# Retention in streamed 128-token units, GpSimd pass rewritten, engine orders pinned: a kernel of attention and ELU feed-forward on one core

## The chip, the cores and the metric

One core of a Trainium2 chip. The time is that of one execution on the device in microseconds (us), as the median of the runs that are quoted with it. "Span" is the time from the first to the last instruction of the profiled execution, and is about 2 us shorter than the time of that execution.

The engines: PE is TensorE, PEld its weight loads, DVE is VectorE, ACT is ScalarE, POOL is GpSimd, SP is the engine whose queue issues most DMAs. PSUM is the memory that the kernels use for matmul results. The lines "L308" in the profile are source lines of the kernel whose profile it is, so they differ from kernel to kernel.

## The reference

```python
# q, k, v: [8 batches, 8 heads, 576 positions, 64], fp32
scores = (1/8) * q @ k^T
ret    = scores * D      # D[i,j] = gamma_h ** (i-j) for i >= j, otherwise 0;  gamma_h = 1 - 2**(-5-h)
attn   = ret @ v                                   # no softmax
x      = attn, heads side by side                  # [4608 tokens, 512]
h      = x @ w_in                                  # w_in [512, 2048]
g      = where(h > 0, h, exp(min(h, 0)) - 1)       # ELU
out    = g @ w_out                                 # w_out [2048, 512] -> [4608, 512] fp32
```

There is no softmax, so the decay gamma^(i-j) can be split into a factor of the query's position and one of the key's position, and a causal sum over earlier keys can be carried as a 64 x 64 state for each head.

## The kernel before

It handles attention in whole batches of 576 positions, head pair by head pair. Python generators weave its steps between the feed-forward matmuls of earlier tokens; a scheduler picks the order on each engine. The parts that matter here (cuts are marked):

```python
    ps_h = ctx.enter_context(tc.tile_pool(name="ps_h", bufs=3, space=PSUM))
    # ... one buffer for the output sums, one for transposes, two for scores, one for values

        def prep(hp):                       # decay folded into q and k, before the transposes
            nc.vector.tensor_tensor(qn, r["q"]..., gq[...], ALU.mult)
            nc.gpsimd.tensor_tensor(kn, r["k"]..., gk[...], ALU.mult)
            nc.scalar.copy(vn.transpose([0, 2, 1, 3]), r["v"])
        # ... nine transposes per head pair on TensorE, copied out of PSUM by ScalarE

    def ffn1(g, ft):                        # 4 matmuls, 512 tokens wide
        # ...
        e = epool.tile([P, TG], FP32, name="e", tag="e")
        nc.scalar.activation(e, ph, AF.Exp)
        nc.gpsimd.tensor_scalar_add(e, e, -1.0)                       # the GpSimd ELU pass
        gt_ = gpool.tile([P, TG], BF16, name="g", tag="g")
        nc.vector.scalar_tensor_tensor(gt_, ph, 0.0, e, ALU.max, ALU.min)
    # ...
    pending = {0: load(0)}                  # a whole batch, then w_in, then attention of batch 0
    for n in range(DF // 512):
        w_in_piece(n, cast)
    for _ in attn(0, pending.pop(0)):
        pass
    # ... w_out; then for each group of 512 tokens: 16 x (ffn1, ffn2 of the group before, attention steps)
```

The GpSimd pass may add -1 to exp(h) for any h, because the last step takes min(max(h, 0), exp(h) - 1): for positive h this is h, since exp(h) - 1 is above it.

## Time and profile before

| | before |
|---|---|
| median (4 runs) | 432.0 us (431.05 to 433.13) |
| span of the profiled run | 429.6 us |
| TensorE busy | 367.1 us, 85% |
| GpSimd busy | 264.5 us, 62% |
| first feed-forward matmul | 40.7 us |

The page of the kernel before, its parts 1, 2 and 4. Part 2 cuts the span into 40 slices of 10.7 us; a digit is the busy share of a slice in tenths, PEclk the granted TensorE clock in tenths.

```profile
span 429.6 us, 6300 instructions
...
PE 367.1 (85%) x2176; PEld 162.5 (38%) x2176; DVE 226.6 (53%) x408; ACT 197.2 (46%) x388; POOL 264.5 (62%) x240
...
PE   0017959998999998999999999999999999999975
...
PEclk9999999998999999999999999999999999999999
DMA  8999789809416837655555331100010001101011
...
PE 48%; POOL 18%; DMA 11%; DVE 9%; issue 7%; ACT 6%; SPq 1%; POOLq 0%; ACTq 0%; DVEq 0%
```

The start is plain to see: three slices in which TensorE does little and DMA is busy. After that TensorE is nearly full, but the chain of waits (last line) does not run through it alone: 18% of the span is GpSimd.

Part 5, the groups of instructions: line, engine, operation, output<-input, shapes, count, then busy us, mean ns of one, and idle time before them with what ended it.

```profile
L295 POOL TENSOR_SCALAR e<-e 128x512 f32<-128x512 f32 x144 | 215.2, 1498 | 84.7 <-ACT e L294 82.8
L297 DVE SCALAR_TENSOR_TENSOR g<-ph,e 128x512 bf16<-128x512 f32 x144 | 99.4, 691 | 136.3 <-POOL e L295 136.2
```

One GpSimd pass takes 1.5 us, and VectorE sits idle 136 us in all until such a pass is done.

The timeline of TensorE near the end (start us, length us, instruction), where only the feed-forward is left:

```profile
356.41 1.03 PE L290 MATMUL ph<-xt,w_in_sb 128*128 128x512 bf16 x4
357.28 1.03 PE L308 MATMUL pm<-w_out_sb,g 128*128 128x512 bf16 x4
358.14 1.03 PE L290 MATMUL ph<-xt,w_in_sb 128*128 128x512 bf16 x4
```

The starts are 0.865 us apart, so a 512-wide matmul costs 216 ns. (The length shown, 1.03 us, runs on past the next start; the profile models the ends of matmuls, so the starts are what is read here.) 1152 such matmuls, 249 us, are in both kernels.

### The profile page before, as it was taken

The numbers are of one execution on the slowest core, as the hardware profiler recorded it, in microseconds if no ns is written. First come the engines' busy times: TensorE is split into PE (matmuls) and PEld (weight loads), VectorE is DVE, ScalarE is ACT, GpSimd is POOL, SyncE is SP. The second block draws the span as 40 slices with busy tenths as digits, with TensorE's granted clock in tenths as the row PEclk, the third lists the DMA queues.
The fourth block names the chain that finished last, engine by engine and source line by source line (L and its number), as shares of the span: only waits on it lengthen the run. The fifth ranks groups of instructions, "written<-read, shape, count | busy, mean of one in ns | idle before, by whom it ended". The sixth has DMA issues, their size and how long they took to land.

```text
span 429.6 us, 6300 instructions
## 1 busy us (share of the span) xinstructions
PE 367.1 (85%) x2176; PEld 162.5 (38%) x2176; DVE 226.6 (53%) x408; ACT 197.2 (46%) x388; POOL 264.5 (62%) x240
## 2 busy tenths in 40 slices
PE   0017959998999998999999999999999999999975
PEld 0003414433444444443444444444444444444432
DVE  2326547767655665657566656665555544433310
ACT  2244446663445444545454455455544444434411
POOL 3311239887666776686667666766565558888810
PEclk9999999998999999999999999999999999999999
DMA  8999789809416837655555331100010001101011
GB/s 220 288 260 286 194 223 223 155 0 196 97 29 147 185 96 175 147 139 132 137 122 136 85 89 49 51 24 2 24 50 25 2 25 50 44 31 49 24 58 65
DMA packets 123871, 46.55 MB, mean 108 GB/s; under 512 B 115136, under 2 KB 115136, under 8 KB 123840
## 3 DMA queue, kind: packets, MB, share of 16 engines
q1 hardware_dynamic: 119232, 37.76, 37.4%
q10 hardware_dynamic: 4608, 8.39, 6.3%
q8 instruction: 17, 0.28, 0.3%
q14 instruction: 14, 0.11, 0.1%
HBM read 36.70 MB, written 9.44 MB: 107 GB/s over the span
## 4 chain that ended last, share of the span: by engine, by line
PE 48%; POOL 18%; DMA 11%; DVE 9%; issue 7%; ACT 6%; SPq 1%; POOLq 0%; ACTq 0%; DVEq 0%
PE ph L290 19%; POOL e L295 17%; PE pm L308 15%; PE sc L231 5%; DVE pt L239 5%; ACT e L294 3%; DMA rq<-in_q_dram 2%; DMA wst<-in_moe_w_in_dram 2%; DMA rv<-in_v_dram 2%; DMA wst<-in_moe_w_out_dram 2%; DVE g L297 1%; DMA rk<-in_k_dram 1%; ACT xt L167 1%; ACT ot L313 1%; DMA rt<-in_k_dram 1%
## 5 line engine op out<-in xcount | busy, mean ns | idle before, releaser
L295 POOL TENSOR_SCALAR e<-e 128x512 f32<-128x512 f32 x144 | 215.2, 1498 | 84.7 <-ACT e L294 82.8
L297 DVE SCALAR_TENSOR_TENSOR g<-ph,e 128x512 bf16<-128x512 f32 x144 | 99.4, 691 | 136.3 <-POOL e L295 136.2
L290 PE MATMUL ph<-xt,w_in_sb 128*128 128x512 bf16 x576 | 162.5, 389 | 2.0 <-DVE g L297 1.4
L308 PE MATMUL pm<-w_out_sb,g 128*128 128x512 bf16 x576 | 149.5, 381 | 3.0 <-ACT ot L313 2.9
L294 ACT ACTIVATE e<-ph 128x512 f32<-128x512 f32 x144 | 86.3, 599 | 102.7 <-PE ph L290 100.9
L308 PEld LDWEIGHTS <-g 128*128 128x128 bf16 x576 | 55.5, 98 | 69.1 <-issue 7.9
L290 PEld LDWEIGHTS <-w_in_sb 128*128 128x128 bf16 x576 | 48.9, 99 | 53.6 <-issue 11.2
L231 PE MATMUL sc<-qkT 64*128 64x320 bf16 (+4 forms) x320 | 43.1, 261 | 18.8 <-DVE pt L239 17.3
L191 POOL TENSOR_TENSOR kn<-rk,gk 128x512 bf16<-128x512 f32 x32 | 33.8, 1056 | 24.2 <-DMA rk<-in_k_dram 18.0
L239 DVE TENSOR_TENSOR pt<-sc,mask_136 128x512 bf16<-128x512 f32 x64 | 41.7, 684 | 1.2 <-PE sc L231 1.0
L239 DVE TENSOR_TENSOR pt<-sc,mask_135 128x448 bf16<-128x448 f32 x64 | 37.2, 619 | 6.3 <-PE sc L231 5.6
L231 PEld LDWEIGHTS <-qkT 64*128 64x128 bf16 x320 | 17.1, 96 | 51.6 <-issue 46.4
L313 ACT COPY ot<-pm 128x512 f32<-128x512 f32 x36 | 21.2, 588 | 31.2 <-PE pm L308 31.2
L186 DVE TENSOR_TENSOR qn<-rq,gq 128x512 bf16<-128x512 f32 x32 | 26.9, 846 | 10.8 <-DMA rq<-in_q_dram 1.9
L196 ACT CAST vn<-rv 128x512 bf16<-128x512 f32 x32 | 19.8, 620 | 12.4 <-PE o_1345 L260 0.9
L202 POOL MEMSET qkT<- 128x64 bf16 x32 | 4.8, 153 | 31.0 <-PE o_370 L256 6.2
L220 PE MATMUL st<-vn,kn 128*128 128x128 bf16 x64 | 9.6, 232 | 16.2 <-ACT vn L196 16.2
L220 PEld LDWEIGHTS <-kn 128*128 128x128 bf16 x64 | 6.4, 105 | 22.6 <-issue 17.7
L127 DVE CAST w_in_sb<-wst 128x512 bf16<-128x512 f32 x8 | 3.9, 486 | 16.5 <-DMA wst<-in_moe_w_in_dram 16.5
L206 PEld LDWEIGHTS <-qn 128*128 128x128 bf16 x64 | 5.1, 100 | 17.5 <-DVE qn L186 12.4
L260 PEld LDWEIGHTS <-vn 128*64 128x64 bf16 x128 | 5.8, 111 | 15.4 <-issue 15.3
L127 ACT CAST w_in_sb<-wst 128x512 bf16<-128x512 f32 x8 | 4.9, 618 | 14.2 <-DMA wst<-in_moe_w_in_dram 14.2
(459 smaller groups left out, 242.2 us busy)
## 6 DMA issues: line engine op xcount, KB each, us to landing
rv<-in_v_dram SPq DMA_DIRECT2D x72, 128.0 KB, 3.2
out_dram<-ot SPq DMA_DIRECT2D x36, 256.0 KB, 2.1
rq<-in_q_dram SPq DMA_DIRECT2D x64, 128.0 KB, 3.2
rk<-in_k_dram SPq DMA_DIRECT2D x64, 128.0 KB, 3.1
wst<-in_moe_w_in_dram ACTq DMA_DIRECT2D x16, 256.0 KB, 5.0
wst<-in_moe_w_out_dram ACTq DMA_DIRECT2D x16, 256.0 KB, 3.6
rt<-in_q_dram SPq DMA_DIRECT2D x8, 128.0 KB, 3.7
rt<-in_k_dram SPq DMA_DIRECT2D x8, 128.0 KB, 4.1
```

Source lines behind the costliest of these rows:

```text
L186: nc.vector.tensor_tensor(qn, r["q"].transpose([0, 2, 1, 3]), gq[:, :, h0 : h0 + 2].unsqueeze(3).to_broadcast([P, FT, 2, D]), ALU.mult,)
L191: nc.gpsimd.tensor_tensor(kn, r["k"].transpose([0, 2, 1, 3]), gk[:, :, h0 : h0 + 2].unsqueeze(3).to_broadcast([P, FT, 2, D]), ALU.mult,)
L196: nc.scalar.copy(vn.transpose([0, 2, 1, 3]), r["v"])
L220: nc.tensor.matmul(st, kn[:, t], vn[:, t], start=(t == 0), stop=(t == 1))
L231: nc.tensor.matmul(sc[i][:, o : o + hi - lo], qkT[r, 1, kt * P : (kt + 1) * P], qkT[r, 0, lo:hi], start=True, stop=True,)
L239: nc.vector.tensor_tensor(p, sc[i], mask, ALU.mult)
L290: nc.tensor.matmul(ph, w_in_sb[:, j, ft * P : (ft + 1) * P], xt[:, j], start=(j == 0), stop=(j == KJ - 1))
L294: nc.scalar.activation(e, ph, AF.Exp)
L295: nc.gpsimd.tensor_scalar_add(e, e, -1.0)
L297: nc.vector.scalar_tensor_tensor(gt_, ph, 0.0, e, ALU.max, ALU.min)
L308: nc.tensor.matmul(pm, gts[g, ft][:, it * P : (it + 1) * P], w_out_sb[:, ft], start=(ft == 0), stop=(ft == NFT - 1))
L313: nc.scalar.copy(ot, pm)
```

## The change

The intent: fewer attention matmuls, most transposes off TensorE, a cheaper GpSimd pass, a feed-forward that starts early, and an order on every engine that is written down instead of scheduled. In both kernels the feed-forward matmuls and the bytes of inputs and outputs are the same.

- Attention runs in 36 units of 128 tokens, all eight heads of a unit at once. Within a unit there is a 128 x 128 causal block; what came before enters through a running state in PSUM.
- The decay of the key's position goes into v (GpSimd multiply), that of the query's position into the copy out of PSUM (VectorE multiply). q and k are only cast.
- The q and k of units 0 to 9 are turned (transposed) by TensorE, those of units 10 to 35 by DMA transposes on the SP queue.
- The GpSimd pass is written as (e - 1) x 1 with bf16 output.
- Feed-forward groups are 4, 2, then seven times 4, and 2 units. The first two groups have their second product in half-width pieces, so that it can begin with half of w_out.
- `manual_schedule` pins the order of each engine to the order in the program.

The core of the diff, with cuts:

```diff
+    GROUPS = [[0, 1, 2, 3], [4, 5]] + [list(range(6 + 4 * i, 10 + 4 * i)) for i in range(7)] + [[34, 35]]
+    PE_TURNED = 10
+    ctx.enter_context(tc.manual_schedule())
...
+    def turn(u):
+        if u < PE_TURNED:
+            ps = ps_h.tile([P, 2, HP, P], BF16, name="tr", tag="ph")
+            ... 8 transposes on TensorE
+            nc.vector.tensor_copy(t[:, 0], ps[:, 0])
+            nc.scalar.copy(t[:, 1], ps[:, 1])
+        else:
+            nc.sync.dma_start_transpose(...)
...
+    def stretch(u, ahead=True):          # one unit, its successor's scores ahead of it
+        if ahead:
+            scores(u + 1)
+        inter(u)                         # state x queries
+        state(u)                         # add this unit's keys and values to the state
+        intra(u)                         # masked scores x values
+        if ahead:
+            masks(u + 1)
+        put_x(u)
+        state_out(u)
...
-        nc.gpsimd.tensor_scalar_add(e, e, -1.0)
+        m = epool.tile([P, 512], BF16, name="m", tag="m")
+        nc.gpsimd.tensor_scalar(m[:, :n], e[:, :n], -1.0, 1.0, ALU.add, ALU.mult)
...
+    def ffn2_half(u, c):                 # half the output columns of one unit
+        ...
+        ot = opool.tile([P, 256], FP32, name="oth", tag="ot")     # opool has 3 buffers
+        (nc.scalar.copy if u % 2 else nc.vector.tensor_copy)(ot, pm)
+        nc.sync.dma_start(out[u * P : (u + 1) * P, c * 256 : c * 256 + 256], ot)
...
+    dummy(18)                            # matmuls on zeros
+    prep(0); turn(0); scores(0); masks(0)
+    prep(1); turn(1); stretch(0); prep(2); turn(2); stretch(1); prep(3)
+    cast_w_in(0, [A, G, A, G])
+    turn(3); stretch(2); stretch(3, ahead=False)
+    cast_w_in(1, [A, G, A, G])
+    ... 16 x ffn1(0), with unit 4 and the rest of w_in
+    ... ffn2_half(0..3, 0), with unit 5
+    ... 16 x ffn1(1); ffn2_half(0..3, 1); units 6 to 9
+    for g in range(2, NG + 1):           # the main loop
+        ... ffn1(g, .) and ffn2(g - 1, .) in turn, after every eighth step
+        ... prep(u + 3), load, stretch(u)
```

(Calls that stand on lines of their own in the program are joined with semicolons here.)

## The prediction

It was made from the profile of the kernel before and the diff, without a run of the changed kernel.

> **What bounds the kernel now.** The chain of waits gives 48% of the span to TensorE, 18% to GpSimd, 11% to DMA, 9% to VectorE. Three stages (busy slices, timeline):
> - 0 to 62 us: loading. DMA engines 90 to 100% busy at about 250 GB/s; the first feed-forward matmul starts at 40.7 us, the first GpSimd ELU pass at 62.2.
> - 62 to 350 us: feed-forward with attention woven in, a batch every 43 us. TensorE shows 93%, but the chain hops between GpSimd passes (1.49 us each, 144 of them), masks and evictions in scheduler order.
> - 355 us to the end: pure feed-forward, 216 ns per 512-column matmul. 1152 of them are 249 us: the floor that stays.
> At that rate a 512-token group is 27.6 us; a batch pays 15 us over it for attention.
>
> **What the change does.**
> 1. Attention in 36 units of 128 tokens with a running state: fewer score columns. Transposes of 26 units leave TensorE (their copies leave ScalarE) for DMA. Per unit 40 small matmuls remain, on 64-wide tiles. In the trace such tiles overlap: four attention-value matmuls of 768 columns took 0.29 us up to the next matmul, where in series they need 0.32 plus about 0.1 us for the change of tile shape. Estimate: 1.5 us per unit (1.1 perfectly overlapped, 2.2 issue-bound); 26 units (39 us) lie in the steady stage.
> 2. VectorE per unit: one cast (0.69), a 1024-wide mask (1.2), output scaling (0.69), four ELU minima (0.69 each): 5.4 us of a period of 8.4. ScalarE about 3.4. Neither binds.
> 3. GpSimd pass: two-operation form writing bf16. The Trainium skill's "GPSIMD Engine Reference", section "Performance versus the Vector engine", has 512 elements in 769 ns at best; the trace has 1490 for the one-operation form, 605 for a cast. I expect 0.75 us (confidence 0.65). At 1.5, GpSimd carries 7 of 8.4 us: not the bound in the middle, about 8 us lost at the start.
> 4. DMA transposes, 256 KB each: "DMA: Bandwidth & Descriptors", section "Latency and other measured facts", states 261 GB/s, so (estimate) 1 us plus a fixed cost, beside 4.4 us of loads and stores per unit. Issued three units ahead: hidden.
> 5. Start: pinned load order, TensorE warmed. Ten units and all weights (16.3 MB) at 250 GB/s are down at 66 us; feed-forward starts at about 20 us, and by 74 us some 34 us of it are done.
>
> **Sum.** 74 (start) + 249 - 34 (remaining feed-forward) + 39 (units) + 5 (stalls) + 3 (tail) = 336 us span, 3 more as timed (432.9 against a span of 429.6): about **338 us**; 8 in 10: 320 to 364. Faster by over 2%: 0.96; within: 0.02; slower: 0.02.
>
> **What would show it.** Right: chain of waits over 75% TensorE, almost no GpSimd; GpSimd passes at 0.7 to 0.9 us; TensorE nearly without idle time in the middle, eight feed-forward steps plus one unit every 8.4 us; the main loop beginning at 70 to 80 us, start DMA-bound. Wrong: small matmuls spaced at 50 ns or more (unit over 2.2 us); GpSimd still at 1.5; TensorE waiting for transposed tiles.
>
> **What would make it wrong.** DMA transposes several times dearer (over 4 us of all DMA engines per unit) would starve loads and push past 400; in-order queues making VectorE wait for the current unit's scores or values and delay the ELU minima beyond the three PSUM buffers; issue-bound small matmuls; a lower clock.

## The result and the profile after

| | before | after |
|---|---|---|
| median of 4 runs | 432.0 us (431.05 to 433.13) | 364.5 us (363.85 to 365.93) |
| span of the profiled run | 429.6 us | 363.3 us |
| TensorE busy | 367.1 us | 312.0 us |
| mean granted clock | 0.996 | 0.943 |
| start of the main loop | (none) | 107.4 us |

The ratio after over before is 0.8447, with a 95% interval of 0.8419 to 0.8475. The kernel is faster by 15.5%, in the predicted direction, but 26 us slower than predicted and just outside the range.

The page after, the parts that answer to those above:

```profile
span 363.3 us, 7067 instructions
...
PE 312.0 (86%) x2721; PEld 164.0 (45%) x2754; DVE 199.8 (55%) x312; ACT 141.7 (39%) x264; POOL 136.2 (37%) x218
...
PE   6467759378639999998999899899989999999985
...
PEclk9657999679959999999999999999999999999999
DMA  9999999905999997779497676857222221000111
GB/s 178 247 385 211 263 280 215 246 6 125 204 209 225 208 190 159 165 171 197 103 193 149 145 164 157 169 138 157 60 60 60 60 60 57 31 29 29 60 59 58
...
PE 32%; issue 25%; DVE 17%; POOL 15%; DMA 5%; ACT 3%; SPq 1%; POOLq 0%; DVEq 0%; ACTq 0%
```

A slice is now 9.1 us. The first twelve slices are the ones to look at: TensorE between 3 and 9 tenths, the clock as low as 5 tenths in places, and one slice (the ninth, 73 to 82 us) in which DMA moved only 6 GB/s. From the thirteenth slice on TensorE is full at full clock.

The groups that answer to those of before, each shape by itself:

```profile
L308 POOL TENSOR_SCALAR m<-e 128x512 bf16<-128x512 f32 x128 | 79.6, 623 | 153.2 <-ACT e L306 148.5 <-DVE g L310 2.2 <-DMA rqk<-in_q_dram 1.1
L310 DVE SCALAR_TENSOR_TENSOR g<-ph,m 128x512 bf16<-128x512 f32 x128 | 87.4, 688 | 95.0 <-POOL m L308 94.9
```

The GpSimd pass fell from 1.50 to 0.62 us. VectorE still waits for it, but in the main loop (107.5 to 300 us) these waits are 68.2 us over 96 passes, 0.7 us each, and no TensorE wait on the result is listed there: they are slack.

The stretches of the kernel after: length, then busy us (and instructions) of PE, PEld, DVE, ACT, POOL, then clock, DMA share, GB/s.

```profile
0.00:50.00 50.00, 33.42 (x288) 17.32 (x290) 23.74 (x57) 23.21 (x41) 21.61 (x42) 0.80 1.07 264
50.00:107.50 57.50, 35.09 (x458) 27.47 (x458) 30.46 (x53) 18.54 (x40) 15.54 (x26) 0.85 0.87 173
107.50:300.00 192.50, 186.10 (x1641) 90.18 (x1666) 124.31 (x168) 78.40 (x140) 82.67 (x119) 0.99 0.69 142
300.00:363.30 63.30, 57.41 (x337) 29.05 (x341) 21.30 (x37) 21.50 (x44) 16.41 (x32) 1.00 0.12 46
```

In the first 107.5 us TensorE was busy for 68.5 us, some of it at a reduced clock; in the 192.5 us after that for 186.1 us. The loss against the prediction is therefore to be sought in the start. The terms of the predicted sum, beside what the profile shows:

| term | predicted | measured | difference |
|---|---|---|---|
| start of the main loop | 74 | 107.4 | +33 |
| feed-forward then left | 214 (249 - 34) | 214 (the same groups were done) | 0 |
| 26 units in the loop | 39 (1.5 each) | 30 (1.14 each) | -9 |
| stalls and tail | 8 | 12 (what is left of the span) | +4 |
| timed (median) minus span (profiled run) | 3 | about 1 | -2 |

The cost of a unit is read from the loop's timeline. TensorE, one period:

```profile
149.36 0.42 PE L204 MATMUL sc<-qkT 64*64 64x128 bf16 x16
149.61 0.39 PE L230 MATMUL o<-qkT,sb 64*64 64x128 bf16 x8
149.94 0.32 PE L247 MATMUL st<-vn,qkn 128*64 128x64 bf16 x8
150.08 0.39 PE L264 MATMUL o<-pt,vn 128*64 128x128 bf16 x8
...
157.42 0.42 PE L204 MATMUL sc<-qkT 64*64 64x128 bf16 x16
```

The period is 8.06 us; eight feed-forward steps of 0.865 us are 6.92 us of it, so a unit of 40 small matmuls costs 1.14 us, and no instruction between shows an idle time before it. The loop ran better than predicted. The start was mis-sized: in the list of TensorE the main loop begins here, 33 us after the predicted 74.

```profile
107.44 0.59 PE L301 MATMUL ph<-xt,w_in_sb 128*128 128x512 bf16 x1 [1.14 <-DVE xt L277]
```

### What the start looks like

Four places in the trace of the kernel after, in order of time.

**Units 0 to 3, up to 28.5 us.** Each unit passes through one chain, and the chains hardly overlap. The timeline of unit 2, lines of other engines left out; the bracket gives the idle time before the instruction and what ended it:

```profile
15.90 0.42 DVE L167 CAST qkn<-rqk 128x512 bf16<-128x512 f32 x1
...
16.37 1.04 PE L188 MATMUL tr<-ident,qkn 128*128 128x128 bf16 x8 [1.48 <-DVE qkn L167]
...
17.45 0.42 DVE L189 COPY qkT<-tr 128x512 bf16<-128x512 bf16 x1 [1.13 <-PE tr L188]
17.91 0.59 ACT L190 COPY qkT<-tr 128x512 bf16<-128x512 bf16 x1 [2.51 <-DVE qkT L189]
...
18.54 0.64 PE L204 MATMUL sc<-qkT 64*64 64x128 bf16 x16 [1.14 <-ACT qkT L190]
...
19.24 1.22 DVE L213 TENSOR_TENSOR pt<-sc,mask 128x1024 bf16<-128x1024 f32 x1 [1.37 <-PE sc L204]
...
21.04 0.42 DVE L167 CAST qkn<-rqk 128x512 bf16<-128x512 f32 x1
```

Cast, transposes, a copy by VectorE, then a copy by ScalarE that does not start until the VectorE copy has ended although the two read different halves of the tile, then scores, mask, scaling, and only then the next unit's cast: 5.1 us from one cast to the next. No wait for a load stands in this chain. The first feed-forward matmul starts at 28.5 us; about 20 was expected.

**The first group alone, 28.5 to 50 us.** There is no second product yet to alternate with. Each of three PSUM buffers goes through TensorE, ScalarE, GpSimd and VectorE before it comes free: 12 matmuls start at 41.12 and the next at 44.32, so three steps take 3.20 us, 1.07 us each instead of 0.86. Weight casts run on the same engines; what they add was not measured.

```profile
41.12 2.75 PE L301 MATMUL ph<-xt,w_in_sb 128*128 128x512 bf16 x12 [0.84 <-DVE g L310]
...
44.32 0.81 PE L301 MATMUL ph<-xt,w_in_sb 128*128 128x512 bf16 x3 [0.45 <-DVE g L310]
```

**A store that waited for loads, 59 to 70 us.**

```profile
65.31 1.08 SPq L347 DMA_DIRECT2D out_dram<-oth  x1
...
69.31 0.37 ACT L346 COPY oth<-pmh 128x256 f32<-128x256 f32 x1 [10.19 <-DMA out_dram<-oth]
...
69.74 1.01 PE L301 MATMUL ph<-xt,w_in_sb 128*128 128x256 bf16 x4 [5.11 <-ACT oth L346]
```

ScalarE sat 10.2 us before the fourth half-width output, since the three output buffers were full and the first store (65.31) stood in the SP queue behind the backlog of loads. Behind ScalarE the exponentials and then TensorE stood still.

**Units 6 to 9, 82 to 107 us,** and the hand-over to DMA transposes:

```profile
101.12 1.42 SPq L192 DMA_TRANSPOSE qkT<-qkn  x1
...
104.87 0.64 PE L204 MATMUL sc<-qkT 64*64 64x128 bf16 x16 [5.72 <-DMA qkT<-qkn]
```

Here the scores of the units come 3.3 to 5.2 us apart. Up to 93 us four half-width products run between them, after that nothing does, and the first DMA transpose is waited for in full.

Two theories follow. **A: the start is bound by latencies**, that is by chains of dependent instructions in a pinned order with few buffers; loads keep up. **B: the start is bound by DMA**, as the prediction had it, only with a lower rate than expected. A rival inside A is the granted clock: TensorE ran at half speed in parts of the start. Theory A has several parts, so it was tested part by part; each expectation says what its theories expect of that run.

### The profile page after: what moved, and what is told of

Its sections match the earlier page's. It is cut to its first block, busy times and chain, and to the rows that moved or that the text cites. A ratio compares the mean times of both kernels' runs of the same rounds, so it can differ in the third digit from the quotient of the medians.

```text
span 363.3 us, 7067 instructions
## 1 busy us (share of the span) xinstructions
PE 312.0 (86%) x2721; PEld 164.0 (45%) x2754; DVE 199.8 (55%) x312; ACT 141.7 (39%) x264; POOL 136.2 (37%) x218
## 4 chain that ended last, share of the span: by engine, by line
PE 32%; issue 25%; DVE 17%; POOL 15%; DMA 5%; ACT 3%; SPq 1%; POOLq 0%; DVEq 0%; ACTq 0%
PE pm L322 13%; PE ph L301 13%; POOL m L308 12%; DVE pt L213 6%; DVE qkn L170 3%; DVE xt L277 3%; DVE g L310 2%; POOL vn L176 2%; DMA rqk<-in_q_dram 2%; PE sc L204 2%; PE tr L188 1%; ACT qkT L190 1%; DMA rqk<-in_k_dram 1%; DMA qkT<-qkn 1%; PE pmh L341 1%
## 5 line engine op out<-in xcount | busy, mean ns | idle before, releaser
L310 DVE SCALAR_TENSOR_TENSOR g<-ph,m 128x512 bf16<-128x512 f32 (+1 forms) x160 | 100.7, 635 | 121.9 <-POOL m L308 121.8
L301 PE MATMUL ph<-xt,w_in_sb 128*128 128x512 bf16 (+1 forms) x616 | 150.1, 367 | 20.3 <-DVE xt L277 7.0
L308 POOL TENSOR_SCALAR m<-e 128x512 bf16<-128x512 f32 (+1 forms) x160 | 92.8, 582 | 192.2 <-ACT e L306 186.4
L306 ACT ACTIVATE e<-ph 128x512 f32<-128x512 f32 (+1 forms) x160 | 88.5, 555 | 147.9 <-PE ph L301 143.2
L322 PE MATMUL pm<-w_out_sb,g 128*128 128x512 bf16 x503 | 129.3, 381 | 2.6 <-ACT ot L332 1.6
L213 DVE TENSOR_TENSOR pt<-sc,mask 128x1024 bf16<-128x1024 f32 x36 | 43.7, 1215 | 11.3 <-PE sc L204 11.3
L176 POOL TENSOR_TENSOR vn<-rv,gk 128x512 bf16<-128x512 f32 x36 | 37.5, 1044 | 13.8 <-DMA rv<-in_v_dram 6.5
L204 PE MATMUL sc<-qkT 64*64 64x128 bf16 x576 | 15.9, 232 | 13.3 <-ACT qkT L190 7.5
L277 DVE TENSOR_TENSOR xt<-o,gx 128x512 bf16<-128x512 f32 x36 | 24.4, 678 | 2.9 <-PE o L264 2.9
L170 DVE CAST qkn<-rqk 128x1024 bf16<-128x1024 f32 x26 | 23.0, 888 | 0.0
L264 PE MATMUL o<-pt,vn 128*64 128x128 bf16 x288 | 15.5, 233 | 1.6 <-DVE pt L213 1.6
L190 ACT COPY qkT<-tr 128x512 bf16<-128x512 bf16 x10 | 5.9, 586 | 14.6 <-DVE qkT L189 14.6
```

Of the source, the lines that this page charges most:

```text
L170: eng(n, src)
L176: nc.gpsimd.tensor_tensor(n, rv, gk[:, u % R].unsqueeze(2).to_broadcast([P, H, D]), ALU.mult)
L204: nc.tensor.matmul(sc[j * 64 : (j + 1) * 64, i, hp], t[r, 1, hp, j * 64 : (j + 1) * 64], t[r, 0, hp], start=(hp == 0), stop=(hp == HP - 1) ...
L213: nc.vector.tensor_tensor(pt.rearrange("p i h t -> p (i h) t"), scs[u].rearrange("p i h t -> p (i h) t"), m.unsqueeze(1).to_broadcast([P, ...
L264: nc.tensor.matmul(o[i * D : (i + 1) * D, hp], vns[u][:, h], pts[u][:, i, hp], start=(u % R == 0 and hp == 0), stop=(hp == HP - 1), skip_g ...
L277: nc.vector.tensor_tensor(xts[g][:, :, i * P : (i + 1) * P], os_[u], gx[:, :, s0 : s0 + P], ALU.mult)
```

## The experiments

Unless said otherwise the kernels are edits of the kernel after, have correct outputs, and ran in three rounds beside the kernel before. "Loop" is the start of the main loop on TensorE in the profiled run (107.4 us in the kernel after). The kernel before had medians of 431.2 to 432.6 us in these rounds. Differences of 1 to 2 us between two of these kernels lie within the intervals of their ratios (in square brackets), so they are at the edge of what these runs can tell.

### Five buffers for the half-width outputs

```diff
-    opool = ... bufs=3
+    opool = ... bufs=2
-        e = epool.tile([P, 512], FP32, name="e", tag="e")
+        e = epool.tile([P, 512], FP32, name="e", tag="e", bufs=3)
-        ot = opool.tile([P, 256], FP32, name="oth", tag="ot")
+        ot = opool.tile([P, 256], FP32, name="oth", tag="oth", bufs=5)
```

> The changed kernel, but the half-width output tiles of the first group get five buffers of their own (the full-width ones keep two of three, the exponential tiles three of four, to fit). Theory A (the start is lost to engine order and to buffers): the fourth half-width copy no longer waits 10 us on ScalarE for a store that stands behind the backlog of loads; TensorE's idle stretch at 65 to 70 us goes, the second feed-forward group runs at full clock, the main loop starts 9 to 13 us earlier, time 352 to 356 us. Rival B (the start is bound by DMA as the prediction said): the wait only moves to the next load or weight piece, gain under 3 us, time over 361.

Measured: 360.22 us, ratio 0.8331 [0.8290, 0.8372], loop 103.3. ScalarE's wait before the half-width outputs in this kernel (us in all, times, longest):

```profile
ACT oth L346 <- PE pmh L341: 12.6, 4, 6.7
```

The wait for the store (10.2 us once) is gone from the list; in its place ScalarE waits for the products themselves, 12.6 us where it was 7.1. The gain is 4 us, about half of the least expected: the wait was real, but behind much of it stood the next link of the chain.

### Two more units turned on TensorE

`PE_TURNED = 12`, with `turn(10)` and `turn(11)` placed before the loop, so that the exposed DMA transpose disappears.

> The changed kernel, with units 10 and 11 transposed on TensorE too, so that the first DMA transposes are needed a unit or two later. Theory A: the 5.7 us that TensorE waits for the first DMA transpose at 99 to 105 us go, and with them the half clock after it; 4 to 8 us faster, 357 to 361 us. Rival B (DMA-bound start): the load of the units is what comes late, gain under 2 us.

Measured: 363.23 us, 0.8401 [0.8364, 0.8439], loop 104.9. The start gains 2.6 us and the total 1 to 2, where 4 to 8 were expected: a miss. The 5.72 us wait is gone; in its place TensorE waits for the units' own chain (1.96 us for a cast, 1.20 us for a copy).

### The next unit's cast ahead of the mask

The casts of units 1 to 3 are put before the mask of the unit ahead of them on VectorE, so that they no longer queue behind it.

```diff
-    stretch(0)
-    prep(2)
+    stretch(0, then=lambda: prep(2))     # runs between scores and the rest of the unit
```

> The changed kernel, with the cast of the next unit put before the mask of this one on VectorE for units 1 to 3, which breaks the serial cycle cast, transpose, two copies, scores, mask of 5.1 us a unit. Theory A: units 0 to 3 follow at 3.6 to 4 us (then bound by their loads), the first feed-forward starts 3 to 5 us earlier than 28.5 us; of that 1 to 4 us reach the end, 360 to 363 us. Rival B: units follow the loads already, nothing changes (under 1 us).

Measured: 365.31 us, 0.8449 [0.8417, 0.8481]; the first feed-forward matmul 1.0 us earlier, loop 106.9. No gain in the total, where 1 to 4 us were expected.

### All three together

> The three edits together, and units 8 to 10 cast early too. Theory A: the gains add up, 20 to 28 us, time 337 to 345 us, main loop from about 80 to 86 us; its length (from there to the end, 256 us) does not change by more than 3 us. Rival B: all that is left is the DMA-bound start, total gain under 5 us.

The edit is the three above plus the earlier cast for units 8 to 10. Measured: 355.72 us, 0.8229 [0.8195, 0.8262], loop 98.6. The gain is 8.8 us; 20 to 28 were expected. The parts had given 4, 1 and 0 alone; the rest of the 8.8 belongs to the three acting together or to the fourth edit, which was not run alone. Either way most of the expected gain did not come: more links were still in the chain, as the runs below show.

### DMA or latency: the same bytes in wide rows (a wrong result, on purpose)

The loads of q, k and v read 256-byte rows (64 fp32 of one head). Here they read 2 KB rows of the same tensor, the same number of bytes in an eighth of the rows. The data land in wrong places, so the result is wrong.

```diff
-                nc.sync.dma_start(dst, src[b, :, s0 : s0 + n, :].rearrange("h p d -> p h d"))
+                nc.sync.dma_start(dst.rearrange("p h d -> p (h d)"), src[b].rearrange("h (r e) d -> (h r) (e d)", e=8)[s0 : s0 + n])
```

> Wrong result on purpose: the mended kernel, with every unit of q, k and v read as rows of 2 KB instead of eight pieces of 256 B, the same bytes and destinations. Rows of 2 KB move at about 310 GB/s by the weights of the kernel before, against about 220, so ten units take about 10 us less of DMA. Theory A: the main loop starts at most 4 us earlier than in the mended kernel (98.6 us), time 352 to 356. Rival B (DMA-bound start): it starts 8 to 11 us earlier, time 345 to 348.

Measured, on top of the kernel of three edits: 351.85 us, 0.8143 [0.8110, 0.8176], loop 94.5. That is 4 us faster than the same kernel with narrow rows, with the first feed-forward matmul 3.5 us earlier (24.2 for 27.7). The loads did become much cheaper: the last load of the tenth unit is issued at 45.3 us instead of 60.7, and from 60 to 70 us DMA moves 13 GB/s instead of 221. Yet the loop begins only 4.1 us earlier. So loads 15 us sooner are worth about 4 us of the excess of 33. Theory B in its strong form falls; a small share for DMA stays, mostly in the first units.

### The second group interleaved

`ffn1` of the second group alternates with the second halves of the first group's outputs, and units 6 to 10 are woven between instead of following.

> The mended kernel (all three edits), with the second feed-forward group, the second halves of the first group's outputs and units 6 to 10 interleaved one step at a time, instead of one after the other. Theory A (the stretch from 64 to 99 us is bound by the latency of dependency chains that nothing overlaps: 3.7 us a unit, 0.7 us a feed-forward step that costs TensorE 0.43): main loop from 86 to 92 us instead of 98.6, time 343 to 350 us against 355.7. Rival B (loads bind it): main loop from 97 or later, gain under 2 us.

Measured: 354.61 us, 0.8198 [0.8165, 0.8230], loop 95.7. The loop begins 2.9 us earlier, but the total gains only 1.1: an expectation missed (343 to 350). In the trace of this run the units come every 5.4 us. VectorE, which casts, copies, masks and scales them in program order, is busy 4.0 us of each (74.8 to 80.2 us), TensorE 4.5, and VectorE waits 1.43 us once a unit for the GpSimd pass. No engine is full: the stage is still a chain, one that runs through VectorE and GpSimd.

### A fourth PSUM buffer in the first groups

`ps_m`, which has nothing to do while a first product runs alone, serves as the fourth buffer of the first two groups.

```diff
-        ph = ps_h.tile([P, 512], FP32, name="ph", tag="ph")
+        fourth = g < 2 and ft % 4 == 3
+        ph = (ps_m if fourth else ps_h).tile([P, 512], FP32, name="ph", tag="pm" if fourth else "ph")
```

> The mended kernel, with the idle output bank as a fourth buffer for the first products of the first two feed-forward groups, which run without second products between them. In the trace three buffers return every 3.2 us (exponential 0.60, GpSimd pass 0.62, minimum 0.69, about 0.5 of waits, after 0.86 of matmul), so a step of 0.86 us takes 1.07 us, and a half-width step of 0.43 takes 0.72. Theory A (latency of the chain): 3 to 7 us faster than the mended kernel's 355.7, so 349 to 353. Rival B (DMA): under 1 us. Rival C (the casts of the weights on the same engines bind these groups, not buffers): 0 to 2 us.

Measured: 352.49 us, 0.8163 [0.8136, 0.8189], loop 94.7; 3.2 us less than the kernel of three edits. One more buffer is worth 3 us in 32 steps.

### q and k transposed into two PSUM tiles

```diff
-            ps = ps_h.tile([P, 2, HP, P], BF16, name="tr", tag="ph")
+            ps = [ps_h.tile([P, HP, P], BF16, name="tr", tag="ph") for _ in range(2)]
```

> The mended kernel, with the two halves of a transposed unit in two PSUM tiles, so that the copy of k on ScalarE no longer waits for the copy of q on VectorE (the trace has 14.6 us of such waits over ten units). Theory A: 0.45 us off the chain of each of the units that are on the path, 2 to 5 us in all, 351 to 354. Rival B: under 1 us.

Measured: 352.79 us, 0.8157 [0.8119, 0.8194], loop 96.3; 2.9 us less. The waits of ScalarE for its copy, in this kernel:

```profile
ACT qkT L190 <- PE tr L188: 5.9, 7, 2.0
```

In the kernel of three edits this copy waited 15.5 us for the VectorE copy (14.6 in the kernel after). With a tile each, it waits for TensorE only. So it was the shared tile, or the PSUM buffer that it fills, that put the two readers in a row (the edit separates both). The Trainium skill, "PSUM — Partial Sum Buffer", section "PSUM bank collisions raise a hardware error", says that the scheduler of the compiler's back end adds a dependency between any two instructions on different engines that touch the same bank and quadrant of partitions, reads included. The trace agrees: both copies read all 128 partitions of one tile, and they ran one after the other ten times of ten. Who put the wait in, the compiler or the framework that tracks the tiles, no run here shows. The page could have told this before the first run; the prediction did not ask it.

### All start edits

The three edits, the interleaving, the fourth buffer (first group), the split tile, and the first cast of w_in after unit 3 instead of before its copies. No load is changed.

> All start edits together: mended, interleaved second group, fourth buffer for the first group, split transposed tile, and the cast of the first weight piece moved behind unit 3. Not a byte less is loaded. Theory A: main loop from 86 to 92 us, time 342 to 349. If the start is bound by loads (B) it stays at 353 or more.

Measured: **347.48 us** (346.54 to 348.12), 0.8044 [0.8015, 0.8073], correct; first feed-forward matmul at 22.9 us, loop 90.6. This is the fastest version here, 17 us under the kernel after, and it still begins the loop 16.6 us later than predicted:

```profile
90.63 0.58 PE L304 MATMUL ph<-xt,w_in_sb 128*128 128x512 bf16 x1 [1.11 <-DVE xt L277]
```

### The clock kept up

The fastest version with dummy matmuls in the waits of the first 50 us, so that TensorE is never idle for long.

> The kernel with all start edits, with small batches of dummy matmuls where TensorE waits in the first 50 us (where the granted clock was 0.50 to 0.79). If the lowered clock costs time of its own: granted clock above 0.9 there, the first halves of the second product take 3.5 us instead of 6.3, 2 to 5 us faster than 347.5. If the chains on the other engines decide, the clock goes up but the time stays within 1 us, or the dummies delay real work and it is slower.

Measured: 348.88 us (346.66 to 349.80), 0.8069 [0.8021, 0.8117], loop 89.5. First the stretches of the version without dummies, then with them (the number after the five engines is the clock):

```profile
10.00:20.00 10.00, 6.88 (x128) 5.01 (x129) 6.97 (x12) 3.91 (x8) 3.12 (x3) 0.58 1.25 274
20.00:27.00 7.00, 5.26 (x33) 2.64 (x35) 2.06 (x4) 3.50 (x7) 2.95 (x5) 0.50 1.06 388
```

```profile
10.00:20.00 10.00, 7.62 (x138) 4.35 (x139) 6.13 (x11) 3.54 (x7) 3.13 (x3) 1.00 1.16 233
20.00:27.00 7.00, 6.41 (x59) 2.88 (x55) 3.12 (x5) 3.94 (x8) 3.55 (x6) 1.00 1.05 390
```

The clock rose from 0.58 and 0.50 to 1.00. The loop began 1.1 us earlier and the time did not fall (the runs of the two kernels overlap). So the low clock explains little of the length. The test is not quite pure, since the dummies take time on TensorE and one of the three PSUM buffers, and it was made on the fastest version alone. The Trainium skill, "TensorE: Matmul & The Clock Gate", section "What's actually happening", has half rate as the default that activity lifts; the rise from 0.50 to 1.00 with the dummies agrees. It also puts the cost of the ramp at the start below 1% of a typical span; the stretch at half clock is longer here, and lifting it still gained nothing.

### The GpSimd pass alone, in both kernels

The new form put into the kernel before:

```diff
-        nc.gpsimd.tensor_scalar_add(e, e, -1.0)
+        m = epool.tile([P, TG], BF16, name="m", tag="m")
+        nc.gpsimd.tensor_scalar(m, e, -1.0, 1.0, ALU.add, ALU.mult)
```

> The kernel before with only the GpSimd pass of the ELU in its new form (add and multiply, bf16 out). If that pass alone carried much of the gain (the chain of waits gave GpSimd 18% of 430 us): 395 to 415 us. If TensorE and the small attention steps bind the kernel before: 425 or more.

Measured: 414.26 us, 0.9584 [0.9549, 0.9619]: 18 us less. In the chain of waits of this kernel TensorE now has 73%, where it had 48%, and GpSimd 4%, where it had 18%:

```profile
PE 73%; DMA 8%; issue 7%; POOL 4%; DVE 4%; ACT 2%; SPq 1%; ACTq 0%; POOLq 0%; DVEq 0%
```

The old form put back into the kernel after:

> The changed kernel with the old form of the pass (one add, fp32 in place, 1.49 us). The prediction said that it would cost about 8 us, at the start only, since the middle has 7 of 8.4 us for GpSimd: 370 to 376 us. If the pass is on the path in the main loop too: over 385.

Measured: 382.52 us, 0.8847 [0.8814, 0.8880]: 18 us more, with the loop at 115.8 us. The start lost 8 us, as the prediction had said of a slow pass, and the loop lost 9 (265.1 us for 255.9), which it had not; the time lies between the two ranges expected. In the stretch of the main loop GpSimd was not full:

```profile
115.00:315.00 200.00, 188.50 (x1661) 90.17 (x1661) 123.73 (x167) 77.17 (x138) 166.21 (x118) 0.99 0.66 137
```

GpSimd is busy 166 of 200 us, yet from the loop's start to the end TensorE waits 9.7 us for the last scaling before a group and 2.7 us for minima, against 5.4 and none in the kernel after: 7 of the 9 us (one such wait, 1.94 us, is at 181.75 us). GpSimd also has the unit's v multiply, 1.04 us, in its order; how much of the lateness comes from it was not tested. Here an engine that was 83% busy cost time although it was not full.

### Which part of the new form makes it fast

Four forms of the pass by turns in one kernel, one run (368.12 us).

> The changed kernel with four forms of the GpSimd pass in turn, on equal tiles: two operations to bf16, one operation to bf16, two operations to fp32 in place, one operation to fp32 in place. If the second operation makes it fast: 0.62, 1.49, about 0.62, 1.49 us. If the output type does: 0.62, 0.62, 1.49, 1.49. Time between 364 and 383 us.

The GpSimd groups of that kernel at full width, where m_two_bf and m_one_bf are the two with bf16 output, L315 the form with two operations in place in fp32, and L318 the old form:

```profile
L318 POOL TENSOR_SCALAR e<-e 128x512 f32<-128x512 f32 x32 | 47.8, 1494 | 32.5 <-ACT e L306 32.5
L312 POOL TENSOR_SCALAR m_one_bf<-e 128x512 bf16<-128x512 f32 x32 | 47.6, 1488 | 34.1 <-ACT e L306 34.1
...
L309 POOL TENSOR_SCALAR m_two_bf<-e 128x512 bf16<-128x512 f32 x32 | 20.3, 635 | 33.5 <-ACT e L306 33.4
L315 POOL TENSOR_SCALAR e<-e 128x512 f32<-128x512 f32 x32 | 20.1, 628 | 4.3 <-ACT e L306 4.1 <-DMA qkT<-qkn 0.2
```

Two operations are 2.3 to 2.4 times faster than one, and the output type makes no difference. Why, no run here shows.

### Transposes all on TensorE

`PE_TURNED = 36`, each unit turned two units ahead in the loop.

> The changed kernel with all 36 units transposed on TensorE (eight matmuls and two PSUM copies a unit). A unit's eight transposes take 0.44 us of TensorE at full rate and a PSUM buffer of the three; 26 units: TensorE alone 11 us plus mode and buffer waits. Theory (the transposes by DMA are hidden in the main loop): 376 to 392 us. Rival (their traffic costs as much as it saves): within 4 us of 364.5.

Measured: 374.20 us, 0.8661 [0.8610, 0.8713], loop 105.3. The loop takes 267.5 us instead of 255.9, so 24 units turned on TensorE cost 11.6 us in it, 0.48 us each. So the DMA transposes are worth 9.7 us in all, 2 us less than the least expected. The eight transposes of a unit take TensorE 0.45 us from start to start (82.54 to 82.99 us in the kernel after), so the gain in the loop is all of their time, and the DMA transposes cost nothing there that shows.

### Order left to the scheduler

The kernel after without `manual_schedule`.

> The changed kernel without pinned orders: the scheduler orders each engine again. If the pinned order is worth what the change's author thought, the main loop gets waits again and the time is 370 to 400 us; if the scheduler finds a better start (it can pull ready work forward), it may come out at 350 to 364.

Measured: 360.88 us, 0.8356 [0.8327, 0.8386]: faster than the pinned order. The loop begins at 96.2 us instead of 107.4 and takes 263.0 us instead of 255.9. The pinned order wins 7 us in the regular loop and loses 11 in the start, the very part that it was written out for by hand.

## Why the prediction was right or wrong

**The direction and the mechanisms were right.** Attention in units costs TensorE less, the GpSimd pass became cheaper and the DMA transposes are hidden in the loop. From the loop's start to the end the sum was 262 us and the trace has 255.9.

**The step that failed is step 5, the term "74 (start)" of the sum.** The prediction reasoned: "Ten units and all weights (16.3 MB) at 250 GB/s are down at 66 us; feed-forward starts at about 20 us, and by 74 us some 34 us of it are done." The first half came true: the last load of the tenth unit was issued at 61.1 us, which with the median landing time of 4.6 us gives about 66 (an estimate). But the loads were not what bound most of the start. The loop began at 107.4 us, 33 us later than the term. The edits of the fastest version, which change not a byte of the loads, moved the loop to 90.6 us and the time by 17 us, while loads that came 15 us sooner, in wide rows, were worth about 4 us. What ran in the start were chains of dependent instructions: 5.1 us per unit, three steps in 3.2 us for a product alone with three buffers, one store behind queued loads. The prediction asked what DMA could bring and did not walk one unit through its engines.

**The clock explains little of it.** It was low in the start (0.80 and 0.85 in the two stretches), and "TensorE warmed" was wrong: the 18 dummy matmuls at the beginning did not keep it up. But on the fastest version the run with the clock restored gained nothing. The kernel after was not run that way.

**The unit's cost was over-estimated:** 1.14 us measured, 1.5 predicted, close to the 1.1 given for perfect overlap. This hid 9 us of the error; with it right, the prediction would have been 329 us.

**The GpSimd pass was better than expected,** 0.62 us for 0.75, and it is worth 18 us in either kernel. The statement that at 1.5 us GpSimd would not bind "in the middle" was wrong by 9 us.

**Step 2, VectorE, was right for the loop and wrong for the start.** In the loop VectorE is busy 124.3 of 192.5 us and no wait on it recurs within a group; the only regular one is at the change of groups, about 1 us for the last scaling before the next group. In the start it is the engine on which each unit's cast, copy, mask and scaling stand one behind the other.

**The signature "chain of waits over 75% TensorE" failed** (32%, "issue" 25%), although the loop is TensorE-bound: there TensorE is busy 186.1 of 192.5 us. A chain that is followed back through in-order engines with little slack may run along any of them, so its shares are no measure of the bound here. The busy share of the stage said it, and agreed with the period of 8.06 us.

**What stays open:** 16.6 us between the fastest version's loop start (90.6 us) and the 74 us. The first group starts 3 us later than the 20 predicted, and most of the rest lies between 59 and 91 us, where VectorE works through units 6 to 10 in order, one every 4 to 6 us. Loads may still have a part: before 92 us GpSimd waits three times, 7.9 us in all, for a load of v, and wide rows were not tried on this version. One piece of it can be read from the trace of that version: a 512-wide cast on VectorE takes 0.42 us by itself, and 0.92 us where it falls on GpSimd's multiply of v.

```profile
62.03 1.04 POOL L176 TENSOR_TENSOR vn<-rv,gk 128x512 bf16<-128x512 f32 x1
```

```profile
62.44 0.92 DVE L167 CAST qkn<-rqk 128x512 bf16<-128x512 f32 x1
```

The cast ends 0.29 us after the multiply has ended. The next pair, at 66.03 and 66.43 us with the same lengths, does so after 0.28 us. The Trainium skill, "SBUF — State Buffer", section "Who interferes with whom", describes a port pair that VectorE and GpSimd share as an exclusive lock, held for a whole instruction, which casts can take; these lines agree with it. No run moved the multiply away, so its share of the 16.6 us is not shown.

## What to carry to other kernels

Size a start by walking one piece of work through all its engines, with the durations of the trace and the number of buffers, and only then ask whether the bytes arrive in time: a load that is on time says nothing about the chain behind it. When a start is bound by such a chain, each link that is taken away gives back only part of its wait, since the next link is right behind it; here three edits gave 4, 1 and 0 us alone and 8.8 together with a small fourth, and it took four more edits to reach 17. An order pinned by hand paid here in the regular loop and lost in the irregular start, so the two are worth comparing stage by stage.

## What the Trainium skill lacked or had wrong

- "GPSIMD Engine Reference", section "Performance versus the Vector engine", gives 769 ns as the best case for 512 elements, which the two-operation form beats, and does not set one operation of a tensor-scalar instruction against two (its model per element draws a line between a k of 2 and of 3, without saying what k is). The runs show 0.62 to 0.64 us with two operations and 1.49 to 1.50 us with one, for bf16 and fp32 output alike.
- "DMA: Bandwidth & Descriptors", section "Latency and other measured facts", gives the bandwidth of DMA transposes but no latency of one (only a fixed cost of about 2 us for DMAs in general). Here the 26 of 256 KB each landed 3.2 us after issue (median; 3.0 to 5.7), and each took 1.24 us of the SP queue at the median.
- "TensorE: Matmul & The Clock Gate" gives idle gaps of more than about 3.4 us as the rule for what lowers the clock (section "HAM oscillation — how this bites in real kernels"), and names frequent short gaps as a second way without a number (section "A second HAM failure mode: psum-queue depth-cycling"). In the fastest version the clock fell to half between 11.5 and 12 us. From 7 to 12 us TensorE was busy for 2.9 of 5.0 us, 1.7 us of them transposes, and no idle time listed before a matmul exceeded 0.9 us. The page says (section "Part 4: PE-mode transpose") that transposes do not count as busy in the same way, which may be why; it has no figure for the share of activity that keeps the clock up.
